# Block-causal attention and a maxout layer on one core: the rounding remainder of the weights taken by GpSimd, their loads issued by SyncE, two pairs of heads turned by TensorE

## The chip, the cores and the metric

The kernel runs on one core of a Trainium2 chip. The metric is the device time of one execution in microseconds (us). Before the change three runs gave 911.82, 914.31 and 915.15 us, median 914.31 us. Engines are named as in the profile: PE is TensorE, DVE is VectorE, ACT is ScalarE, POOL is GpSimd, SP is SyncE.

## The reference

Inputs are q, k, v of shape (8, 8, 576, 64) and four weight matrices. Attention is causal by blocks of 64 positions; its output, laid out as 4608 tokens of 512 numbers, goes through a layer that takes the largest of three products, and through an output product.

```python
scores = scale * np.matmul(q, k.transpose(0, 1, 3, 2))
scores = np.where(block_i >= block_j, scores, -1000000000.0)
attn = np.exp(scores - np.max(scores, axis=-1, keepdims=True))
attn = attn / (np.sum(attn, axis=-1, keepdims=True) + 1e-09)
out = np.matmul(attn, v)
x = out.transpose(0, 2, 1, 3).reshape(B * S, H * D)
h = np.maximum(np.maximum(x @ w1, x @ w2), x @ w3)
return (h @ w_out).astype(np.float32)
```

The weights arrive as 64-bit floats: each number is a low and a high 32-bit word. w1, w2, w3 are 512 x 768, w_out is 768 x 512.

## The kernel before, in words

**Attention.** Work goes by pairs of heads: 8 batches of 4 pairs. Batch 0 is done twice over, as FRONT pairs (the first 256 positions) and BACK pairs (the rest), so there are 36 pairs in all, numbered from 0 here. For each pair q and k are loaded into `nat`, turned so that the head dimension lies on the partitions (`kq`), multiplied (L934, and L941 for the last 64 rows), masked and reduced to a row minimum of the negated scores on DVE (L423), raised to the exponential on ACT (L607, L961), scaled by the inverse of the row sum on POOL or ACT (L441, L439), turned again (`pt` or `pz`), and multiplied with v (L1001). ACT and DVE copy the result out, ACT rounds it (`xh`), POOL takes the remainder (`xl`, through `minus`, L254).

There are two ways of turning. A *plain* pair (FRONT and BACK) is turned by PE: L825 for q and k, L559 and L987 for the probabilities, each a 128 x 128 transpose, and ACT or DVE copies the result out of PSUM (L251, L249). Any other pair (EARLY for batch 1, WHOLE for batches 2 to 7) is turned by DVE in blocks of 32 (L918 for q and k; L630 and L634 for the probabilities), and eight transfers of 200 KB on SP's queue (L642) bring the blocks to their partitions. The q and k of a pair that isn't plain are loaded in pieces of 32 numbers (L894); those of a plain pair in rows of 64 (L876, L882).

**Weights.** 24 units of 128 x 512 weights (18 of w1 to w3, 6 of w_out), class `Unit`, each turn 64-bit floats into a rounded part `h` and a remainder `l`. Per unit: POOL issues the load of 512 KB (L293). ACT takes the absolute value of the high words (`size`, L303). DVE does five steps: `clamp` L309, `shift` L316, `sign` L322, `power` L328 and `rest` L339. They give a float `a` from the high word and a correction `c` from the low word; `c` lies in a tile `left`, of which there is one, so a unit's `rest` must wait until the unit before has been used by PE. ACT rounds `a` to `h` (`high`). PE forms `a - h + c` in PSUM with three products by an identity (`whole`): L346 multiplies `plus`, read as 32-bit float, with `a`; L347 multiplies `less`, the negated identity, with `h`; L348 multiplies `plus` with `c`. ACT copies the sum to `l` (`lower`).

**Layer.** `Chunk` multiplies x with the weights for one half of a batch (256 or 320 columns). Each product is three matmuls (L1119: high x high, low x high, high x low); the maximum is taken on DVE (L1134); the output products are L1185, three matmuls of 512 columns each. Chunks follow each other; within the first one, each unit of weights gives PE 12 matmuls of 256 columns.

**Order of the work.** Nothing is ordered by hand at the engines. Each piece is a `Job` with an estimated cost for each engine that may do it, a rank, predecessors and slots of buffers; `in_order` plays the list through once, always starting the ready job of lowest rank on an idle engine, and writes the instructions in that order. On the chip each engine, SP's queue too, follows its written order and waits where an operand isn't there yet. A job that may run on two engines goes to the one that is free first by the estimates. So a changed cost or an added job moves others nearby.

**Issue of transfers.** Transfers issued by SP and ACT share eight semaphores in turn; each transfer waits until the one eight before it has landed. Transfers issued by POOL have semaphores of their own.

Of the kernel before, what the change touches and what calls it, by code (L numbers as in the profile page):

```python
# [9 lines left out]
F32 = mybir.dt.float32  # L10
F32R = mybir.dt.float32r
I32 = mybir.dt.int32
# [23 lines left out]
LOAD = 540.0  # L36
ASK = 1000.0
# [100 lines left out]
def pe(*cols, least=128):  # L138
    return sum(max(n, least) / 2.4 + 13.5 for n in cols)


def dve(n, fast=False):
    return 68.0 + n / (1.92 if fast else 0.96)


def act(n, psum=True):
    return (52.0 if psum else 88.0) + n / 1.2


def pool(n):  # L150
    return 150.0 + 2.15 * n
# [3 lines left out]
def kernel(  # L155
# [11 lines left out]
    nc = tc.nc  # L167
    B, H, S, D = q.shape
    DM, DF = w1.shape
    DO = w_out.shape[1]  # L170
    P = 128
    assert (S, D) == (576, 64) and H % 2 == 0
    NP = H // 2
# [14 lines left out]
    NEAR = 4  # L188
# [11 lines left out]
    const = ctx.enter_context(tc.tile_pool(name="const", bufs=1))  # L200
# [20 lines left out]


    plus = const.tile([P, P], F32R, name="plus")
    less = const.tile([P, P], F32R, name="less")
    one = att.tile([P, P], F32, name="p0", bufs=slots["p0"])
    make_identity(nc, one)
    nc.scalar.mul(less, one, -1.0)
    nc.scalar.copy(plus, one)

    wh, wl = {}, {}  # L230
# [8 lines left out]
    def job(cost, rank, call, *args, after=(), take=(), give=(), lasts=0.0, moved=0.0):  # L239
        j = Job(cost, rank, lambda eng: call(eng, *args), after, take, give, lasts, moved)  # L240
        jobs.append(j)
        return j
# [10 lines left out]
    def minus(eng, dst, a, b):  # L253
        {"DVE": nc.vector, "POOL": nc.gpsimd}[eng].tensor_tensor(out=dst, in0=a, in1=b, op=ALU.subtract)  # L254


    class Unit:


        def __init__(self, u, src, dst, n, prior, *early, first=None):  # L260
            self.src, self.dst, self.n, self.u = src, dst, n, u
            self.last = n == DO
            rank = DELAY + PACE * u


            self.tag = f"wo{dst}" if self.last else f"w{u}"
            self.temps = (f"wo{u % NF}",) if not self.last else (f"wo{4 + dst % 2}",) if dst < 4 else ("osb", "osb")
            j = self.issued = job(
                {"POOL": ASK},
                rank - 8,  # L270
                self.load,
                after=(prior and prior.issued, first, *(e.sized for e in early if e)),
                take=(self.tag,) if self.last else (),
            )
            j = job({}, 0, lambda eng: None, after=(j,), lasts=MOVE, moved=1600.0)
            j = self.sized = job({"ACT": act(512, False) + 65.0}, rank, self.size, after=(j,), take=self.temps)
            for step, fast in (
                (self.clamp, True),
                (self.shift, True),
                (self.sign, False),  # L280
                (self.power, True),
                (self.rest, False),
            ):
                c = dve(512, fast) + (130.0 if fast else 80.0)
                e = "DVE"
                j = job({e: c}, rank, step, after=(j,), take=("left",) if step == self.rest else (), lasts=c + GAP)
            j = job({"ACT": act(512, False)}, rank, self.high, after=(j,))
            j = job({"PE": 6 * pe(512)}, rank, self.whole, after=(j,), take=("pm",), give=(*self.temps, "left"))
            self.done = job({"ACT": act(512)}, rank, self.lower, after=(j,), give=("pm",))

        def load(self, eng):
            st = moe.tile([P, 1024], F32, name=self.tag, bufs=1).bitcast(I32)
            nc.gpsimd.dma_start(st.rearrange("p (c f) -> p c f", f=2 * self.n), self.src.bitcast(I32))  # L293
            lo_hi = st.rearrange("p (n t) -> p n t", t=2)
            self.low_word, self.high_word = lo_hi[:, :, 0].bitcast(U32), lo_hi[:, :, 1]

# [46 lines left out]
        def whole(self, eng):  # L343

            self.ps = psm.tile([P, 512], F32, name="pm")
            nc.tensor.matmul(self.ps, plus.bitcast(F32), self.a, start=True, stop=False)  # L346
            nc.tensor.matmul(self.ps, less, self.h, start=False, stop=False)  # L347
            nc.tensor.matmul(self.ps, plus, self.c, start=False, stop=True)  # L348

        def high(self, eng):  # L350
            w = moe.tile([P, 2, 512], F32R, name=self.tag, bufs=1)
            self.h, self.l = w[:, 0], w[:, 1]
            if self.last:
                woh[self.dst], wol[self.dst] = self.h, self.l
            else:
                wh[self.dst], wl[self.dst] = (t.rearrange("p (c f) -> p c f", f=P) for t in (self.h, self.l))
            copy(eng, self.h, self.a)
# [4 lines left out]
    units, begun = {}, []  # L362

    def weights():
        u, prior, early = 0, None, []
        for f in range(NF):
            for i, w in enumerate((w1, w2, w3)):
                prior = units[i, f] = Unit(
                    u, w[:, f * P : (f + 1) * P].rearrange("(c p) f -> p c f", p=P), (i, f), P, prior, early[u - NEAR] if u >= NEAR else None, first=begun[min(u + 1, NP - 1)]
                )  # L370
                early.append(prior)
                u += 1
        for f in range(NF):
            prior = units["out", f] = Unit(
                u,
                w_out[f * P : (f + 1) * P, :].rearrange("(c p) f -> p c f", p=P),
                f,
                DO,
                prior,
                early[2 * NF + f],  # L380
                early[u - 2],
            )
            early.append(prior)
            u += 1
# [7 lines left out]
    RUN = 400  # L392
# [20 lines left out]

    WHOLE = Part(((3,), (2, 0)), (1,), (1, 0), S, slice(0, S), slice(0, RUN), True)
    EARLY = Part(((3,), (2, 0)), (1,), (1, 0), S, slice(0, S), slice(0, RUN))

    FRONT = Part(((1, 0),), (), (0,), 256, slice(0, 256), slice(0, 96), plain=True)
    BACK = Part(((3,), (2,)), (), (1,), S, slice(256, S), slice(96, RUN), plain=True)
# [607 lines left out]
    left = {}  # L1026
# [186 lines left out]
    chunks, made = [], []  # L1213

    def plan(b, part, gap):
        nonlocal rank
        pairs = [Pair(b, hp, part, len(made) + hp) for hp in range(NP)]
        for p in pairs:
            p.plan(rank, made[-1] if made else None)
            made.append(p)  # L1220
            rank += gap
        return pairs

    rank = 0
    front = plan(0, FRONT, FRONT_PAIR)
    start = rank + SECOND + 6
    back = plan(0, BACK, BACK_PAIR)
    chunks.append((0, 0, front, start, rank + END))
    start, pairs = rank + END, {0: back}
    for b in range(1, B):  # L1230
        pairs[b] = plan(b, EARLY if b == 1 else WHOLE, PAIR)
        if b == 1:
# [4 lines left out]
        start = rank + END  # L1237
# [5 lines left out]
    prior = None  # L1243
    for b, half, pairs, start, end in chunks:
        prior = Chunk(b, half, pairs, prior, start, end)
# [33 lines left out]
```

## Time and profile before

| what | value |
|---|---|
| median of three runs | 914.31 us |
| the profiled execution | 913.83 us |
| its span, first to last instruction | 912.0 us |
| PE busy | 892.8 us, 98% |
| DVE busy | 529.3 us, 58% |
| ACT busy | 471.7 us, 52% |
| POOL busy | 254.8 us, 28% |
| weight loads, POOL's queue | 18 of w1 to w3 and 6 of w_out, 512 KB each |

The profile gives busy time by engine, the span cut into stretches, groups of equal instructions by line and shape, waits by releaser, and a chain of work followed back from the last instruction. A busy PE can still be late: matmuls are pipelined and a matmul's recorded length runs over the next one's start, so the pace of PE is read from start to start.

### The profile page before, as it was taken

The page shows a single profiled execution, that of the slowest core. Times are in us where ns is not written, and L with a number is a line of the kernel's source. Part 1 is how long each engine was busy: PE and PEld are TensorE (multiplying, and loading weights), DVE is VectorE, ACT ScalarE, POOL GpSimd, SP SyncE. Part 2 cuts the span into 40 slices and gives each one's busy share as a digit, 9 for nine tenths or more (in the row PEclk, how much of TensorE's full clock was granted, in tenths as well). Part 3 has the DMA queues.
Part 4 walks back from the last instruction along what each step waited for, and adds up shares of the span by engine and source line. Part 5 has one row for each costly group of instructions (what it writes and reads, how often), then busy time and mean ns, then how long its engine had stood idle before and what let it go on. Part 6 is the DMA issues. An engine that isn't in the chain of part 4 may idle for free.

```text
span 912.0 us, 16897 instructions
## 1 busy us (share of the span) xinstructions
PE 892.8 (98%) x5880; PEld 743.1 (81%) x5880; DVE 529.3 (58%) x1545; ACT 471.7 (52%) x1365; POOL 254.8 (28%) x381
## 2 busy tenths in 40 slices
PE   6999899999999999999999999999999999999998
PEld 4577677777888888888888888888888888899997
DVE  4999888786545756564555746564554756421111
ACT  3887675666544635545543645546553644522111
POOL 3553232243221312223221322233131322222100
PEclk9899999999999999999999999999999999999999
DMA  5772645776554544454554543555553533330010
GB/s 163 202 217 50 135 116 116 167 150 144 106 135 110 104 101 90 115 118 115 112 130 97 105 108 89 125 113 121 112 123 87 118 82 83 97 73 24 1 36 23
DMA packets 226132, 98.36 MB, mean 108 GB/s; under 512 B 189696, under 2 KB 218368, under 8 KB 226048
## 3 DMA queue, kind: packets, MB, share of 16 engines
q1 hardware_dynamic: 208192, 82.35, 40.6%
q0 software_dynamic: 3456, 12.58, 4.4%
q10 hardware_dynamic: 14400, 2.36, 1.4%
q8 instruction: 46, 0.75, 0.3%
q14 instruction: 38, 0.31, 0.1%
HBM read 41.94 MB, written 9.44 MB: 56 GB/s over the span
## 4 chain that ended last, share of the span: by engine, by line
PE 90%; DVE 5%; DMA 1%; ACT 1%; issue 1%; ACTq 0%; POOL 0%; DVEq 0%
PE pm L1119 50%; PE pm L1185 16%; PE sb L1001 10%; PE sb L934 8%; PE sb L941 3%; PE pm L346 1%; DMA nat<-in_q_dram 1%; DVE sb L423 1%; DVE left L339 1%; DVE wo L322 1%; PE sb L559 1%; DMA nat<-in_k_dram 0%; DVE kq L251 0%; ACT p L439 0%; PE pm L348 0%
## 5 line engine op out<-in xcount | busy, mean ns | idle before, releaser
L1119 PE MATMUL pm<-xh,w 128*128 128x320 f32 (+1 forms) x2304 | 498.6, 303 | 0.7 <-ACT xh L249 0.5
L1119 PEld LDWEIGHTS pm<-xh,w 128*128 128x128 f32 x2304 | 378.8, 189 | 18.8 <-issue 14.0
L1119 PE MATMUL pm<-xl,w 128*128 128x256 f32 (+1 forms) x1152 | 340.7, 296 | 0.5 <-DMA nat<-in_k_dram 0.5
L1119 PEld LDWEIGHTS pm<-xl,w 128*128 128x128 f32 x1152 | 218.5, 190 | 6.7 <-issue 5.3
L423 DVE CUSTOM_DVE_ANT_0 sb<-sb,mask 128x512 f32<-128x512 f32 (+3 forms) x288 | 143.7, 530 | 133.5 <-PE sb L941 76.1
L607 ACT ACTIVATE p<-sb,nm 128x256 f32<-128x256 f32 (+3 forms) x256 | 133.9, 527 | 80.2 <-DVE nm L423 73.7
L1134 DVE TENSOR_TENSOR m<-pm,m 128x256 f32<-128x256 f32 (+1 forms) x192 | 85.9, 448 | 147.9 <-PE pm L1119 147.1
L441 POOL TENSOR_TENSOR p<-p,rs 128x128 f32<-128x128 f32 (+4 forms) x133 | 97.9, 755 | 253.9 <-DVE rs L751 194.5
L630 DVE STREAM_TRANSPOSE pz<-p 128x512 f32<-128x512 f32 (+1 forms) x280 | 137.7, 527 | 36.0 <-ACT p L439 19.1
L254 POOL TENSOR_TENSOR hl<-m,hh 128x256 fp32r<-128x256 f32 x96 | 71.5, 745 | 248.4 <-ACT hh L249 216.5
L1185 PE MATMUL pm<-wo,hh 128*128 128x512 f32 x384 | 119.2, 392 | 0.0
L439 ACT ACTIVATE p<-p,rs 128x512 f32<-128x512 f32 (+4 forms) x155 | 88.2, 597 | 20.6 <-DVE rs L751 14.1
L249 ACT CAST hh<-m 128x256 fp32r<-128x256 f32 x96 | 38.8, 405 | 110.1 <-DVE m L1134 109.1
L934 PE MATMUL sb<-kq 64*128 64x256 f32 (+3 forms) x512 | 89.1, 466 | 3.2 <-DVE kq L251 3.1
L1001 PE MATMUL sb<-pt,vn 128*64 128x320 f32 (+4 forms) x840 | 90.2, 363 | 0.4 <-DVE pt L251 0.3
L254 POOL TENSOR_TENSOR xl<-x,xh 128x256 fp32r<-128x256 f32 (+1 forms) x64 | 52.7, 829 | 130.9 <-ACT xh L249 130.9
L1001 PEld LDWEIGHTS sb<-pt,vn 128*64 128x64 f32 x840 | 55.1, 137 | 34.5 <-issue 1.7
L1185 PEld LDWEIGHTS pm<-wo,hh 128*128 128x128 f32 x384 | 70.9, 188 | 14.9 <-issue 0.3
L934 PEld LDWEIGHTS sb<-kq 64*128 64x128 f32 x512 | 46.3, 192 | 38.1 <-issue 20.8
L1185 PE MATMUL pm<-wo,hl 128*128 128x512 f32 x192 | 74.9, 390 | 0.0
L249 ACT COPY osb<-pm 128x512 f32<-128x512 f32 x36 | 21.1, 587 | 69.5 <-PE pm L1185 67.4
L249 ACT COPY m<-pm 128x256 f32<-128x256 f32 (+1 forms) x96 | 38.1, 397 | 32.6 <-PE pm L1119 23.9
(82 smaller groups left out, 764.0 us busy)
## 6 DMA issues: line engine op xcount, KB each, us to landing
pt<-pz SPq DMA_DIRECT2D x224, 200.0 KB, 3.9
w<-in_moe_w_dram POOLq DMA_DIRECT2D x18, 512.0 KB, 5.2
vn<-in_v_dram SPq DMA_DIRECT2D x64, 128.0 KB, 2.4
out_dram<-osb SPq DMA_DIRECT2D x32, 256.0 KB, 2.0
nat<-in_k_dram SPq DMA_DIRECT2D x112, 72.0 KB, 2.4
nat<-in_q_dram SPq DMA_DIRECT2D x96, 72.0 KB, 2.5
wo<-in_moe_w_out_dram POOLq DMA_DIRECT2D x6, 512.0 KB, 4.4
nat<-in_q_dram ACTq DMA_DIRECT2D x16, 72.0 KB, 4.3
```

What stands on the lines that cost most here:

```text
L249: nc.scalar.copy(dst, src)
L254: {"DVE": nc.vector, "POOL": nc.gpsimd}[eng].tensor_tensor(out=dst, in0=a, in1=b, op=ALU.subtract)
L423: nc.vector.tensor_tensor_reduce(out=ps, in0=ps, in1=hidden, scale=-SCALE, scalar=first, op0=ALU.add, op1=ALU.min, accum_out=out_)
L439: nc.scalar.mul(p, p, r)
L441: nc.gpsimd.tensor_tensor(out=p, in0=p, in1=r.broadcast_to([P, p.shape[1]]), op=ALU.mult)
L607: nc.scalar.activation(dst, src, AF.Exp, bias=nm[:, c : c + 1], scale=-1.0, accum_out=sm[:, c : c + 1])
L630: nc.vector.transpose(dst, p[:, 0 : n * P])
L934: nc.tensor.matmul(ps, self.q[h.own, P * t : P * (t + 1)], self.k[h.own, 0:w], start=True, stop=True)
L1001: nc.tensor.matmul(o[h.own].rearrange("p (i u) -> p i u", u=n)[:, :, c0 : c0 + z - a], self.vn[:, kt, h.j, :], h.pt[:, :, h.off + a : h.of ...
L1119: nc.tensor.matmul(self.ps, w[i, f][:, c, :], xx, start=(c == 0 and s == 0), stop=(c == NC - 1 and s == 2))
L1134: nc.vector.tensor_tensor(out=m, in0=ps, in1=m, op=ALU.max)
L1185: nc.tensor.matmul(self.po[: self.rows], h, w[f], start=(f == 0 and s == 0), stop=(f == NF - 1 and s == 2))
```

## The change

Three edits, in `Unit`, in `weights` and in `plan`.

1. *Remainder.* A new step `remain` on POOL writes `l = a - h` (512 columns, operands in SBUF, through `minus`). PE's `whole` then has two products, `plus` with `l` and `plus` with `c`, both with operands of the rounded format; `plus` is no longer read as 32-bit float, and `less` is gone. `lower` writes the sum over `l` as before.
2. *Loads.* The 24 loads of weights are issued on SP's queue and no longer on POOL's. The planner charges them to SP at 540 ns. The first four are tied to fixed moments (1.5, 4.0, 6.5 and 9.0 us of the planner's time) and no longer to the loads of k of pairs 1 to 3.
3. *Pairs.* The first two pairs of batch 1 are plain (`FIRST`, the same division as `EARLY`), so that PE and not DVE turns them.

```diff
-    less = const.tile([P, P], F32R, name="less")
-    nc.scalar.mul(less, one, -1.0)
...
-                {"POOL": ASK},
+                {"SP": LOAD},
...
             j = job({"ACT": act(512, False)}, rank, self.high, after=(j,))
-            j = job({"PE": 6 * pe(512)}, rank, self.whole, after=(j,), take=("pm",), give=(*self.temps, "left"))
+            j = job({"POOL": pool(512)}, rank, self.remain, after=(j,))
+            j = job({"PE": 2 * pe(512)}, rank, self.whole, after=(j,), take=("pm",), give=(*self.temps, "left"))
...
-            nc.gpsimd.dma_start(st.rearrange("p (c f) -> p c f", f=2 * self.n), self.src.bitcast(I32))
+            nc.sync.dma_start(st.rearrange("p (c f) -> p c f", f=2 * self.n), self.src.bitcast(I32))
...
-            nc.tensor.matmul(self.ps, plus.bitcast(F32), self.a, start=True, stop=False)
-            nc.tensor.matmul(self.ps, less, self.h, start=False, stop=False)
+            nc.tensor.matmul(self.ps, plus, self.l, start=True, stop=False)
             nc.tensor.matmul(self.ps, plus, self.c, start=False, stop=True)
+
+        def remain(self, eng):
+
+            minus(eng, self.l, self.a, self.h.bitcast(F32))
...
-  early[u - NEAR] if u >= NEAR else None, first=begun[min(u + 1, NP - 1)]
+  early[u - NEAR] if u >= NEAR else None, first=job({}, 0, lambda eng: None, lasts=1500.0 + 2500.0 * u) if u < NEAR else None
...
+    FIRST = Part(((3,), (2, 0)), (1,), (1, 0), S, slice(0, S), slice(0, RUN), plain=True)
...
-        pairs = [Pair(b, hp, part, len(made) + hp) for hp in range(NP)]
+        pairs = [Pair(b, hp, FIRST if b == 1 and hp < 2 else part, len(made) + hp) for hp in range(NP)]
```

In the changed kernel line numbers are shifted by one to three: L345 and L346 are the products of `whole`, L292 is the load, L252 `minus`, L308, L315, L321, L327 and L338 the five steps on DVE, L828 the turning of q and k on PE.

SP's queue at the program's start, before. `nat` takes k, `vn_75` and `vn_76` take v of alternate pairs:

```order
L876 DMA nat<-in_k_dram 128x2x64 x2
L903 DMA vn_75<-in_v_dram 128x2x64 x2
L876 DMA nat<-in_k_dram 128x2x64 x2
L903 DMA vn_76<-in_v_dram 128x2x64 x2
L876 DMA nat<-in_k_dram 128x2x64 x4
L903 DMA vn_75<-in_v_dram 128x2x64 x2
```

The same place after; `w_100` is the tile of unit 0, `w_121` of unit 1 and so on:

```order
L879 DMA nat<-in_k_dram 128x2x64 x2
L906 DMA vn_75<-in_v_dram 128x2x64 x2
L292 DMA w_100<-in_moe_w_dram 128x4x256
L879 DMA nat<-in_k_dram 128x2x64 x2
L906 DMA vn_76<-in_v_dram 128x2x64 x2
L292 DMA w_121<-in_moe_w_dram 128x4x256
L292 DMA w_131<-in_moe_w_dram 128x4x256
L879 DMA nat<-in_k_dram 128x2x64 x2
L292 DMA w_159<-in_moe_w_dram 128x4x256
L292 DMA w_164<-in_moe_w_dram 128x4x256
L292 DMA w_190<-in_moe_w_dram 128x4x256
L879 DMA nat<-in_k_dram 128x2x64 x2
```

Six loads of weights now stand among the loads of k and v of the first four pairs; the k of pair 2 follows the loads of units 0 to 2, and further loads stand behind loads of v, which wait for PE to be done with the tile.

DVE's order before, from the inverse of the second pair's row sums to the end of unit 0's conversion (`wo_207` holds unit 0's `a`):

```order
L751 RECIPROCAL rs<-rs 128x2x2
L309 TENSOR_SCALAR wo_207<-wo_207 128x512
L251 COPY kq<-sb 128x2x256
L316 TENSOR_SCALAR wo_207<-wo_207 128x512
L322 SCALAR_TENSOR_TENSOR wo_207<-w_139,wo_207 128x512
L251 COPY pt<-sb 128x2x4x32
L328 TENSOR_SCALAR wo_207<-wo_207 128x512
L251 COPY pt<-sb 128x4x32
L423 ISA sb,nm<-sb,mask 128x256
L423 ISA nm 128x1
L339 SCALAR_TENSOR_TENSOR left<-w_139,wo_207 128x512
```

And after, the end of unit 0's conversion (`wo_151` holds its `a`, `wo_178` that of unit 1):

```order
L315 TENSOR_SCALAR wo_151<-wo_151 128x512
L308 TENSOR_SCALAR wo_178<-wo_178 128x512
L321 SCALAR_TENSOR_TENSOR wo_151<-w_100,wo_151 128x512
L249 COPY kq<-sb 128x2x256
L750 TENSOR_SCALAR rs<-sm 128x2x2
L327 TENSOR_SCALAR wo_151<-wo_151 128x512
L754 RECIPROCAL rs<-rs 128x2x2
L338 SCALAR_TENSOR_TENSOR left<-w_100,wo_151 128x512
L426 ISA sb,nm<-sb,mask 128x256
```

Unit 0 is now converted before the first row minimum of pair 2, and unit 1's first step stands inside it; before, unit 0 ended among the row minima of pair 3.

PE's order before, around the use of unit 1 (`wo_286`), with the scores of the first BACK pair (L934) and the product with v of pair 2 (L1001) ahead of it:

```order
L934 MATMUL sb<-kq 128x512 x2
L934 MATMUL sb<-kq 128x384 x2
L1001 MATMUL sb<-pz,vn_75 64x256 x2
L1001 MATMUL sb<-pz,vn_75 64x4x32 x2
L346 MATMUL pm<-wo_286,plus 128x512
L347 MATMUL pm<-w_416,less 128x512
L348 MATMUL pm<-left,plus 128x512
```

And after (`w_373` is unit 1's remainder from POOL):

```order
L1004 MATMUL sb<-pz,vn_75 64x256 x2
L1004 MATMUL sb<-pz,vn_75 64x4x32 x2
L828 MATMUL sb<-plus,nat 128x128 x7
L345 MATMUL pm<-w_373,plus 128x512
L346 MATMUL pm<-left,plus 128x512
L937 MATMUL sb<-kq 128x512 x2
L937 MATMUL sb<-kq 128x384 x2
```

Three products have become two, and unit 1 is used before the scores of that pair and no longer after them. Over the whole program PE has 68 more transposes, DVE two fewer of L918, 20 fewer of L630, 4 fewer of L634 and 24 more copies of L251, and SP 16 fewer transfers of L642.

More of the change, by code (lines that the diff above doesn't have):

```diff
@@ L368, in weights @@
                 prior = units[i, f] = Unit(
-                    u, w[:, f * P : (f + 1) * P].rearrange("(c p) f -> p c f", p=P), (i, f), P, prior, early[u - NEAR] if u >= NEAR else None, first=begun[min(u + 1, NP - 1)]
+                    u, w[:, f * P : (f + 1) * P].rearrange("(c p) f -> p c f", p=P), (i, f), P, prior, early[u - NEAR] if u >= NEAR else None, first=job({}, 0, lambda eng: None, lasts=1500.0 + 2500.0 * u) if u < NEAR else None
                 )
```

## The prediction

> **What bounds the kernel now.** I read the page first: who is busy, and what the chain of work that ended last is made of.
>
> ```profile
> PE 892.8 (98%) x5880; PEld 743.1 (81%) x5880; DVE 529.3 (58%) x1545; ACT 471.7 (52%) x1365; POOL 254.8 (28%) x381
> PE 90%; DVE 5%; DMA 1%; ACT 1%; issue 1%; ACTq 0%; POOL 0%; DVEq 0%
> ```
>
> Over the whole span PE is the limit. The shares are means, though, and the change touches only the part in which weights are converted. So the windows come next (us, then busy time and instructions of PE, PEld, DVE, ACT, POOL, the clock, DMA share and GB/s).
>
> ```profile
> 0.00:22.80 22.80, 13.95 (x62) 9.74 (x62) 9.61 (x39) 7.97 (x25) 8.74 (x22) 1.00 0.59 163
> 22.80:45.60 22.80, 20.55 (x96) 12.50 (x93) 21.12 (x62) 18.93 (x57) 11.86 (x19) 0.85 0.71 202
> 45.60:68.40 22.80, 22.53 (x143) 16.67 (x145) 21.32 (x51) 19.58 (x51) 12.81 (x16) 1.00 0.75 217
> 68.40:91.20 22.80, 22.75 (x142) 17.43 (x139) 22.18 (x54) 17.57 (x43) 8.28 (x9) 1.00 0.24 50
> 91.20:114.00 22.80, 20.14 (x122) 13.68 (x121) 18.64 (x42) 15.05 (x38) 6.36 (x9) 1.00 0.62 135
> 114.00:136.80 22.80, 22.80 (x137) 16.25 (x136) 19.01 (x54) 17.39 (x50) 6.98 (x8) 1.00 0.50 116
> 136.80:159.60 22.80, 22.36 (x126) 16.89 (x125) 20.30 (x60) 13.57 (x40) 4.61 (x6) 1.00 0.52 116
> 182.40:912.00 729.60, 725.05 (x4923) 622.25 (x4921) 380.60 (x1138) 347.16 (x1022) 189.07 (x286) 1.00 0.44 98
> ```
>
> Three stages differ. To 22.8 us nobody is full: a chain of first loads, scores and exponentials. From 22.8 to 91.2 us DVE is busy for 21.12 + 21.32 + 22.18 = 64.62 of 68.4 us and PE for 65.83: both are limits at once. From 91.2 to 159.6 us DVE is busy for 57.95 us and PE for 65.30. After 182.4 us PE stands still for 4.55 us in 729.6, and no part of the change is there. What can be won lies in the first 160 us.
>
> What fills DVE in the middle stage is the five steps of a unit (groups by shape, 22 to 91 us, mean ns before the last bar):
>
> ```profile
> L322 DVE SCALAR_TENSOR_TENSOR wo<-w,wo 128x512 int32<-128x512 int32 x16 | 11.4, 725 | 0.0
> L339 DVE SCALAR_TENSOR_TENSOR left<-w,wo 128x512 fp32r<-128x512 uint32 x14 | 10.3, 739 | 1.3 <-PE pm L348 1.3
> L316 DVE TENSOR_SCALAR wo<-wo 128x512 int32<-128x512 int32 x16 | 9.3, 596 | 0.0
> L309 DVE TENSOR_SCALAR wo<-wo 128x512 f32<-128x512 f32 x16 | 9.0, 576 | 0.2 <-ACT wo L303 0.2
> L328 DVE TENSOR_SCALAR wo<-wo 128x512 int32<-128x512 int32 x16 | 7.7, 483 | 0.0
> ```
>
> That is 47.7 of 64.62 us, or 3.1 us a unit. None of it is removed by the change.
>
> **The change part by part.** The sum is made against the profiled execution: 913.83 us, its span of 912.0 and 1.83 around it; that is 0.5 us under the median of 914.31.
>
> *The remainder, on PE.* PE's timeline shows a unit's products and what follows, then transposes (start, length).
>
> ```profile
> 105.49 1.02 PE L346 MATMUL pm<-wo,plus 128*128 128x512 f32 x2
> 105.99 0.75 PE L347 MATMUL pm<-w,less 128*128 128x512 f32 x1
> 106.58 0.40 PE L348 MATMUL pm<-left,plus 128*128 128x512 f32 x1
> 106.81 0.28 PE L1119 MATMUL pm<-xh,w 128*128 128x256 f32 x1
> ...
> 111.58 1.09 PE L559 MATMUL sb<-plus,p 128*128 128x128 f32 x7 [0.42 <-ACT p L439]
> 112.50 0.71 PE L987 MATMUL sb<-plus,p 128*128 128x128 f32 x5
> 112.97 0.36 PE L1119 MATMUL pm<-xh,w 128*128 128x256 f32 x1
> ```
>
> From start to start a unit takes 106.81 - 105.49 = 1.32 us. L348, one product of the rounded format, takes 106.81 - 106.58 = 0.23. Two such remain, 0.46, so PE is relieved of 0.86 us a unit: 24 x 0.86 = 20.6 us.
>
> *The two pairs, on PE.* 68 transposes are added. Twelve take 112.97 - 111.58 = 1.39 us, 0.116 each, so 7.9 us. Net relief of PE: 12.7 us. If PE alone set the end, that would be the gain.
>
> *The two pairs, on DVE.* The groups over the whole span give what goes; two copies out of PSUM, from 22 to 91 us, bound what comes.
>
> ```profile
> L630 DVE STREAM_TRANSPOSE pz<-p 128x512 f32<-128x512 f32 (+1 forms) x280 | 137.7, 527 | 36.0 <-ACT p L439 19.1
> ...
> L634 DVE STREAM_TRANSPOSE pz<-p 128x128 f32<-128x128 f32 x56 | 15.1, 269 | 0.0
> L918 DVE STREAM_TRANSPOSE kq<-nat 128x1152 f32<-128x1152 f32 x28 | 38.1, 1361 | 3.4 <-DMA nat<-in_q_dram 3.1 <-PE sb L934 0.2
> ...
> L251 DVE COPY pt<-sb 128x256 f32<-128x256 f32 x5 | 2.1, 416 | 0.0
> L251 DVE COPY kq<-sb 128x512 f32<-128x512 f32 x3 | 2.0, 674 | 0.0
> ```
>
> 20 x 0.527 + 4 x 0.269 + 2 x 1.361 = 14.3 us leave DVE. 24 copies come to it, at 0.416 to 0.674, so 10.0 to 16.2 us: between -4.3 and +1.9. I take -2, since copies of both sizes are among them. The rest goes to ACT, which has 3 to 5 us free in each window. So DVE is hardly relieved, and the 3.1 us a unit stay.
>
> *The remainder, on POOL.* A subtraction of 512 columns isn't in the trace. It is bounded by a product of 512 columns, and by the subtractions of 256 and 320 columns. The load that leaves POOL stands below them:
>
> ```profile
> L441 POOL TENSOR_TENSOR p<-p,rs 128x512 f32<-128x512 f32 x27 | 29.2, 1087 | 4.6 <-PE sb L1001 4.3 <-DVE rs L751 0.4
> L254 POOL TENSOR_TENSOR hl<-m,hh 128x256 fp32r<-128x256 f32 x96 | 71.5, 745 | 248.4 <-ACT hh L249 216.5 <-ACT left L249 31.7
> L254 POOL TENSOR_TENSOR xl<-x,xh 128x320 fp32r<-128x320 f32 x32 | 29.2, 914 | 119.8 <-ACT xh L249 119.8
> ...
> L293 POOL DMA_DIRECT2D w<-in_moe_w_dram x18 | 14.5, 808 | 0.0
> ```
>
> From 1.09 to 0.914 + 3 x (0.914 - 0.745) = 1.42 us; I take the middle, 1.25. POOL gets 24 x 1.25 = 30 us and loses some 24 x 0.81; in its fullest window it was busy for 12.81 of 22.8 us, so its own time is covered. What isn't covered is what it does to DVE. The same step of DVE, alone and beside POOL:
>
> ```profile
> 19.50 0.40 DVE L309 TENSOR_SCALAR wo<-wo 128x512 f32<-128x512 f32 x1
> ...
> 66.53 1.90 DVE L309 TENSOR_SCALAR wo<-wo 128x512 f32<-128x512 f32 x2
> ```
>
> ```profile
> 66.05 3.28 POOL L441 TENSOR_TENSOR p<-p,rs 128x384 f32<-128x384 f32 x3 [1.44 <-DVE rs L751]
> ```
>
> 0.40 us alone, 0.95 each beside POOL. Against 0.40, the means of 0.576, 0.596 and 0.483 above cost 16 x (0.176 + 0.196 + 0.083) = 7.3 us in the middle stage, while POOL was busy for 32.95 us, loads among it: 0.22 us per us. The 16 units of that stage add 20 us of POOL and take away 13, so +1.5 us for DVE if a load counts like a subtraction; if loads count for nothing, 7.3 / (32.95 - 13) x 20 = +7.3. I take +2, since slowed steps are seen beside loads as well. The Trainium skill ("SBUF — State Buffer", Who interferes with whom) says that a DVE instruction in a two-port mode, or with two SBUF inputs, and a GpSimd instruction that reads SBUF shut each other out for the whole instruction. The rows agree in kind; by that rule at its worst the term would be 20 and not 2.
>
> PE's first product of a unit now waits for POOL, and behind it in PE's order stand that unit's matmuls and the next pair's scores. The way from ACT's rounding to PE's end is 1.25 longer by POOL and 0.86 shorter by PE; with one tile `left`, the next `rest` waits for all of it. 0.4 us more, against 3.1 of DVE work a unit, is covered, unless POOL's queue holds a scaling ahead of it: then 1.09 more.
>
> *The loads, on SP.* What each queue showed: SP's longest wait (us, times, longest), the first conversion's steps, and the second load of q for the third pair on ACT's queue.
>
> ```profile
> SPq L903 <- PE sb L1001: 61.3, 6, 22.0
> ...
> 16.33 0.66 ACT L303 ACTIVATE wo<-w 128x512 f32<-128x512 f32 x1
> ...
> 24.80 0.69 DVE L339 SCALAR_TENSOR_TENSOR left<-w,wo 128x512 fp32r<-128x512 uint32 x1
> ...
> 9.58 0.43 ACTq L876 DMA_DIRECT2D nat<-in_q_dram  x1
> ```
>
> Unit 0 was converted at 24.80 us, while DVE had been idle for 13.2 of the first 22.8. By the changed order unit 0 and a step of unit 1 stand ahead of the third pair's row minima; 1.1 units at 3.1 us are at best 3.5 us moved into idle time. Against that, six loads of 0.5 MB come among the first k and v, where 163 GB/s were already moved (2.5 us a load at the 202 to 217 of the next windows), and ACT's loads of q share semaphores with them; ACT stands still while its queue waits. That loses 0 to 4 us. I take -2 for the start, between -3.5 and +4. Unit 6's load is the first behind a v that waits for PE; it is needed six units, 18.6 us of DVE, after unit 0's, so I take nothing for it.
>
> *Fewer transfers.* The first pair that DVE turned waited long for its q:
>
> ```profile
> 91.58 6.70 DMA nat<-in_q_dram
> 98.56 1.38 DVE kq L918
> ```
>
> That wait is on the chain, and PE was busy for only 20.14 us of that window. The first two pairs of batch 1 no longer meet it; a later pair may. I take half, -3.4.
>
> *The sum by stages.* Start: -2. Middle: DVE's 3.78 us of idle time are all that PE's relief can win there; half of it, -1.9, with +2 from POOL: 0. Third stage: PE loses 8 x 0.86 = 6.9 and gains 7.9, +1; DVE -2 and +0.9, on which PE waits in part, -1; the wait -3.4: together -3.4. Total -5.4: 913.83 - 5.4 = 908.4 us. Of PE's 12.7 us the larger part is spent waiting for DVE, which is late next.
>
> **The rivals.**
>
> *PE's relief arrives in full.* For it: PE 90% of the chain, and DVE's copies can go to ACT. Then -12.7: 901.1 us (897 to 904). Against it: 64.62 of 68.4 us of DVE, with nothing taken from it before the pairs of batch 1. Chance 0.22.
>
> *Nothing is left of it.* SP's order decides: weights behind v that waits for PE (61.3 us in six waits, 22.0 the longest), and the first q later, so that the start gives +2 where I took -2, and the wait for q only passes to the next pair (0 for -3.4). 908.4 + 4 + 3.4 = 915.8, say 912 to 918. Against it: v's loads wait because they come early. Chance 0.15.
>
> *Slower, by POOL holding DVE.* In the middle stage DVE wants one of the five steps 47.7 / 64.62 = 74% of the time. If each subtraction stops DVE for its whole 1.25 us, the middle gets 20 instead of 2: 926.4 us. It counts as slower from 0.78 us a unit on, (10.5 + 2) / 16. For it: 0.95 against 0.40. Against it: the mean of L309 was 0.576 beside a POOL that was busy for half of the stage, 32.95 of 68.4 us. Chance 0.13. By the rule of the Trainium skill named above this is what happens whenever POOL is first and DVE wants one of the steps.
>
> **How the numbers follow.** A measurement of this kernel can tell about 0.5%, 4.6 us, from no change: faster is under 909.7, slower over 918.9. My forecast has 0.50; its own range is 903 to 914 (start up to +4 or -3.5, middle -3.8 to +5), and of it 0.31 lies under 909.7, 0.19 above. Faster: 0.31 + 0.22 = 0.53. Same: 0.19 + 0.15 = 0.34. Slower: 0.13. The range goes from 899, into the first rival, to 917, to the end of the second, and leaves out the last and a tip of the first.
>
> **What would show it.** Right: DVE busy for over 66 us of 22.8 to 91.2 us, PE for some 10 less than before; L345 waiting for POOL for less than 0.5 us at a time; unit 0's `rest` (L338) before 22 us; the five steps' means up by less than 0.1 us; the last `whole` between 145 and 152 us. Wrong: PE still full in the middle stage and the last `whole` before 140 us (first rival); ACT or DVE waiting for a load of weights, or for q, for more than 2 us (second); the two-operand steps and L308 near 1 us in the mean (third). After 182 us PE's idle time must stay near 4.6 us; if it grows, the two pairs have been paid for elsewhere, and the sum is wrong in a place where I put nothing.

## The result, and the profile after

The changed kernel took 921.43 us, the median of five runs (917.73 to 924.26), against 914.31 before. The ratio is 1.0079, with a 95% interval of 1.0059 to 1.0100: slower by 7 us, by more than the 0.5% that a measurement can tell. The forecast was 908.4, with a range of 899 to 917. The profiled execution took 919.79 us, its span was 918.0.

The page of the changed kernel, the shares and the chain:

```profile
PE 888.3 (97%) x5900; PEld 743.0 (81%) x5900; DVE 537.5 (59%) x1543; ACT 477.0 (52%) x1375; POOL 269.4 (29%) x378
PE 87%; DVE 6%; ACT 2%; issue 1%; DMA 1%; POOL 1%; ACTq 1%; SPq 0%; DVEq 0%; POOLq 0%
```

In net PE lost 48 instructions of the weights and got 68 transposes (5880 + 20 = 5900). Its share of the chain fell from 90% to 87%: work went away, and waiting came. The windows say where (us; busy time of PE, PEld, DVE, ACT, POOL; clock; DMA share; GB/s):

```profile
0.00:22.80 22.80, 14.18 (x57) 9.21 (x58) 11.65 (x46) 11.62 (x35) 6.21 (x17) 1.00 0.85 247
22.80:45.60 22.80, 17.81 (x89) 10.67 (x87) 20.31 (x56) 15.81 (x47) 10.05 (x11) 0.83 0.54 140
45.60:68.40 22.80, 21.87 (x149) 17.51 (x147) 20.94 (x49) 17.52 (x46) 11.82 (x12) 0.95 0.68 194
68.40:91.20 22.80, 17.81 (x104) 12.86 (x101) 22.46 (x46) 15.65 (x38) 10.00 (x8) 0.93 0.09 26
91.20:114.00 22.80, 19.51 (x139) 14.98 (x138) 21.56 (x48) 18.16 (x45) 11.79 (x10) 1.00 0.37 98
114.00:136.80 22.80, 21.93 (x143) 16.75 (x143) 21.79 (x56) 19.05 (x53) 12.00 (x13) 1.00 0.39 100
136.80:159.60 22.80, 22.63 (x154) 17.07 (x151) 18.95 (x51) 16.28 (x48) 10.67 (x14) 1.00 0.44 98
182.40:918.00 735.60, 730.30 (x4944) 625.92 (x4940) 383.69 (x1150) 349.72 (x1028) 188.59 (x285) 1.00 0.44 98
```

In the middle stage, 22.8 to 91.2 us, PE is busy for 17.81 + 21.87 + 17.81 = 57.49 us, where it was 65.83. DVE is as full as before, 63.71 against 64.62. After it DVE is full for longer: 43.35 us of the two windows from 91.2 to 136.8, where it was 37.65. What DVE did in the middle stage shows in the groups of 22 to 91 us (count; busy us, mean ns):

```profile
L321 DVE SCALAR_TENSOR_TENSOR wo<-w,wo 128x512 int32<-128x512 int32 x13 | 10.8, 828 | 0.0
L308 DVE TENSOR_SCALAR wo<-wo 128x512 f32<-128x512 f32 x13 | 10.2, 786 | 0.0
L338 DVE SCALAR_TENSOR_TENSOR left<-w,wo 128x512 fp32r<-128x512 uint32 x12 | 9.0, 752 | 1.4 <-PE pm L346 1.3
L327 DVE TENSOR_SCALAR wo<-wo 128x512 int32<-128x512 int32 x13 | 8.5, 656 | 0.0
L315 DVE TENSOR_SCALAR wo<-wo 128x512 int32<-128x512 int32 x14 | 7.3, 524 | 0.0
L426 DVE CUSTOM_DVE_ANT_0 sb<-sb,mask 128x512 f32<-128x512 f32 x9 | 6.2, 692 | 0.6 <-PE sb L944 0.6
```

The five steps take nearly the same DVE time as before (45.8 us against 47.7; the last row is the masked reduction, for later), but 13 units instead of 16. DVE is full, and each unit costs it more: L308 went from 576 to 786 ns, L327 from 483 to 656, L321 from 725 to 828. The new instruction on POOL, from the groups of the first 160 us:

```profile
L252 POOL TENSOR_TENSOR w<-wo,w 128x512 fp32r<-128x512 f32 x18 | 26.3, 1462 | 28.1 <-ACT w L247 24.9 <-DMA wo<-in_moe_w_out_dram 3.2
```

It takes 1.46 us where I had 1.25. The start and the end of the conversion, from the timeline (start, length): unit 0's `rest`, and the last unit's last product.

```profile
19.24 0.69 DVE L338 SCALAR_TENSOR_TENSOR left<-w,wo 128x512 fp32r<-128x512 uint32 x1
...
161.10 0.39 PE L346 MATMUL pm<-left,plus 128*128 128x512 f32 x1
```

Unit 0 is 5.6 us earlier than before (24.80), as its earlier load promised. The last unit is outside the 145 to 152 us that I forecast, on the late side: before, it came at 150.71, and in e5 below, the same order without the subtraction, at 148.77.

### The profile page after: what moved, and what is told of

Same layout as the page of the kernel before. It is cut to its first block, busy times and chain, and to the rows that moved or that the text cites. A ratio compares the mean times of both kernels' runs of the same rounds, so it can differ in the third digit from the quotient of the medians.

```text
span 918.0 us, 16954 instructions
## 1 busy us (share of the span) xinstructions
PE 888.3 (97%) x5900; PEld 743.0 (81%) x5900; DVE 537.5 (59%) x1543; ACT 477.0 (52%) x1375; POOL 269.4 (29%) x378
## 4 chain that ended last, share of the span: by engine, by line
PE 87%; DVE 6%; ACT 2%; issue 1%; DMA 1%; POOL 1%; ACTq 1%; SPq 0%; DVEq 0%; POOLq 0%
PE pm L1122 48%; PE pm L1188 16%; PE sb L1004 10%; PE sb L937 8%; PE sb L944 3%; DVE sb L426 1%; DVE left L338 1%; DVE wo L321 1%; PE sb L562 1%; DVE wo L327 1%; DVE wo L308 1%; DMA nat<-in_k_dram 1%; ACT p L610 0%; DMA pt<-pz 0%; ACT w L247 0%
## 5 line engine op out<-in xcount | busy, mean ns | idle before, releaser
L1137 DVE TENSOR_TENSOR m<-pm,m 128x256 f32<-128x256 f32 (+1 forms) x192 | 85.9, 448 | 145.3 <-PE pm L1122 144.4
L444 POOL TENSOR_TENSOR p<-p,rs 128x128 f32<-128x128 f32 (+4 forms) x128 | 93.4, 748 | 244.3 <-DVE rs L754 181.8
L633 DVE STREAM_TRANSPOSE pz<-p 128x512 f32<-128x512 f32 (+1 forms) x260 | 127.8, 528 | 35.5 <-ACT p L442 19.3
L252 POOL TENSOR_TENSOR hl<-m,hh 128x256 fp32r<-128x256 f32 x96 | 72.9, 759 | 233.0 <-ACT hh L247 201.2
L442 ACT ACTIVATE p<-p,rs 128x256 f32<-128x256 f32 (+4 forms) x160 | 91.3, 599 | 15.4 <-DVE rs L754 9.3
L252 POOL TENSOR_TENSOR xl<-x,xh 128x256 fp32r<-128x256 f32 (+1 forms) x64 | 52.6, 828 | 115.2 <-ACT xh L247 111.8
L1004 PEld LDWEIGHTS sb<-pt,vn 128*64 128x64 f32 x812 | 52.7, 138 | 34.2 <-issue 1.9
L937 PEld LDWEIGHTS sb<-kq 64*128 64x128 f32 x512 | 45.8, 192 | 40.8 <-issue 21.3
```

Source lines behind the costliest of these rows:

```text
L442: nc.scalar.mul(p, p, r)
L444: nc.gpsimd.tensor_tensor(out=p, in0=p, in1=r.broadcast_to([P, p.shape[1]]), op=ALU.mult)
L633: nc.vector.transpose(dst, p[:, 0 : n * P])
L937: nc.tensor.matmul(ps, self.q[h.own, P * t : P * (t + 1)], self.k[h.own, 0:w], start=True, stop=True)
L1004: nc.tensor.matmul(o[h.own].rearrange("p (i u) -> p i u", u=n)[:, :, c0 : c0 + z - a], self.vn[:, kt, h.j, :], h.pt[:, :, h.off + a : h.of ...
L1137: nc.vector.tensor_tensor(out=m, in0=ps, in1=m, op=ALU.max)
```

## The experiments

Three theories were set against each other. Theory 1: POOL's subtraction, reading the same memory, takes time from DVE's five steps. Theory 2: the loads on SP spoil the start. Theory 3: the two pairs put more on PE than they take away. Times below are medians; "against before" is the difference to the median of the kernel before on the same chip.

**One edit alone, and two without the first.** Of the diff of the change, e1 has only edit 1 (remainder), e2 only edit 2 (loads), e3 only edit 3 (pairs), e4 edits 2 and 3. As a sample, the whole of e2:

```diff
-                {"POOL": ASK},
+                {"SP": LOAD},
-            nc.gpsimd.dma_start(st.rearrange("p (c f) -> p c f", f=2 * self.n), self.src.bitcast(I32))
+            nc.sync.dma_start(st.rearrange("p (c f) -> p c f", f=2 * self.n), self.src.bitcast(I32))
-  first=begun[min(u + 1, NP - 1)]
+  first=job({}, 0, lambda eng: None, lasts=1500.0 + 2500.0 * u) if u < NEAR else None
```

> The kernel before with the remainder on POOL alone: two products on PE a unit, loads still issued by POOL, no further plain pairs. Theory 1 (POOL's subtraction shuts DVE out of its five steps): slower than before, 917 to 927 us, with L309, L316 and L328 at 0.65 us or more in the mean from 22 to 160 us, although PE has 20.6 us less to do. Theory 2 (the loads on SP spoil the start and hold up q): faster, 898 to 908 us. Theory 3 (the two pairs put too much on PE and ACT): faster, 898 to 908 us.

> The kernel before with the loads of the weights on SP's queue alone. Theory 1: near the kernel before or somewhat faster, 908 to 915 us, since POOL is relieved of 18 us of issuing. Theory 2: slower, 919 us or more, with ACT or DVE waiting for q or for a load. Theory 3: near the kernel before.

> The kernel before with the first two pairs of batch 1 turned by PE alone. Theory 1: within 5 us of the kernel before, 909 to 919 us; PE has 7.9 us more to do, but DVE's wait of 6.7 us for q goes. Theory 2: the same. Theory 3: slower, 919 us or more.

> The changed kernel without the remainder on POOL: loads on SP and two plain pairs, PE forming the remainder in three products as before. Theory 1: faster than the changed kernel by 5 us or more, 906 to 916 us, with the five steps of DVE back near 0.42 and 0.68 us. Theory 2 and theory 3: as slow as the changed kernel or slower, 920 to 932 us, since PE has 20.6 us more to do.

| kernel | us | ratio, 95% interval | against before |
|---|---|---|---|
| e1, remainder alone | 932.20 | 1.0206 (1.0183 to 1.0229) | +18.9 |
| e2, loads alone | 909.87 | 0.9961 (0.9947 to 0.9976) | -3.5 |
| e3, pairs alone | 919.93 | 1.0061 (1.0039 to 1.0083) | +6.6 |
| e4, loads and pairs | 917.18 | 1.0037 (1.0024 to 1.0050) | +3.8 |

Theory 2 falls: the loads on SP win 3.5 us and beat the kernel before. Theory 1 has the right sign in e1, but 932.20 is more than its 917 to 927: this order has a loss of its own, as e12 shows below. L308 and L315 took 701 and 668 ns there, as asked, L327 only 495. e4 is 4.3 us faster than the changed kernel, a little under the 5 that theory 1 asked for, and just over its 906 to 916. Theory 3 holds for the pairs by themselves. The windows of e3 show why:

```profile
91.20:114.00 22.80, 22.32 (x142) 16.52 (x141) 20.45 (x49) 17.38 (x45) 8.98 (x11) 1.00 0.45 129
114.00:136.80 22.80, 22.49 (x140) 16.54 (x139) 18.41 (x51) 17.17 (x48) 7.52 (x10) 1.00 0.37 94
136.80:159.60 22.80, 22.80 (x144) 17.64 (x143) 14.54 (x42) 15.34 (x47) 2.95 (x5) 1.00 0.42 85
159.60:182.40 22.80, 22.80 (x157) 18.88 (x157) 16.11 (x48) 12.49 (x41) 6.93 (x11) 1.00 0.33 56
```

From 91.2 us on PE is full, busy for 22.32 us of the window in which it was busy for 20.14 before. The wait for q is gone, but PE is given 7.9 us of transposes in a place where it has no time for them. And e2, which leaves the pairs to DVE, has this:

```profile
91.20:114.00 22.80, 22.42 (x136) 15.68 (x136) 20.54 (x48) 15.54 (x41) 5.60 (x7) 1.00 0.53 115
114.00:136.80 22.80, 22.80 (x130) 16.40 (x127) 21.51 (x63) 16.20 (x44) 4.91 (x8) 1.00 0.52 119
```

22.42 us: with the loads alone PE's gap in that window has closed as well. There was nothing left in it for the pairs to win.

**What of the remainder costs: PE's new wait or POOL's hold on DVE.** In the next three the changed kernel's order is kept. e5 leaves POOL's subtraction out; e6 lets it write into a tile that nobody reads; e7 puts two fills in its place, so that POOL still stands between ACT and PE but reads nothing. In e5 and e6 PE multiplies `h` where it multiplied `l`.

```diff
 e5
-            nc.tensor.matmul(self.ps, plus, self.l, start=True, stop=False)
+            nc.tensor.matmul(self.ps, plus, self.h, start=True, stop=False)
-            minus(eng, self.l, self.a, self.h.bitcast(F32))
+            pass
 e6, the product as in e5
-            minus(eng, self.l, self.a, self.h.bitcast(F32))
+            minus(eng, spare, self.a, self.h.bitcast(F32))
 e7, the product as in the changed kernel
-            minus(eng, self.l, self.a, self.h.bitcast(F32))
+            nc.gpsimd.memset(self.l.bitcast(F32), 0.0)
+            nc.gpsimd.memset(self.l.bitcast(F32), 0.0)
```

> The changed kernel, POOL's subtraction left out; PE multiplies the rounded part h where it multiplied l (the output is that of a computation without the remainder). PE keeps its relief of 0.86 us a unit. Theory 1 (the subtraction on POOL costs what PE gains): the run comes to 917.2, the time of loads and pairs together, less 12 to 20.6 us of PE: 897 to 905 us; PE nearly full from 45 us on; the five steps of DVE back to the means of before (0.48 to 0.74 us). Rival A (PE's relief is worth nothing, since DVE is full anyway): 914 to 919 us, with DVE over 63 us busy from 22.8 to 91.2 us and PE under 60.

> The changed kernel with POOL's subtraction going into a tile that nobody reads; PE multiplies h where it multiplied l (the remainder is left out of the output). POOL works as in the changed kernel, but PE does not wait for it. Theory 1a (POOL takes DVE's time while it subtracts): 916 to 922 us, as the changed kernel, and the five steps of DVE as slow as there (0.66 to 0.83 us in the middle stage). Theory 1b (the way from ACT over POOL to PE is too long for one tile of corrections): 897 to 906 us, as without the subtraction. Half of each: near 911.

> The changed kernel with two fills of 512 columns in place of POOL's subtraction: POOL still stands between ACT and PE, for about 1 us a unit, but reads no operand (the remainder is left out of the output). Theory 1a (two operands read by POOL shut DVE out): 897 to 906 us and DVE's five steps at the means of before. Theory 1b (the way is too long): 914 to 921 us, with PE waiting for POOL as in the changed kernel.

e5 took 908.33 us (ratio 0.9951, 0.9933 to 0.9969), e6 921.05 (1.0088, 1.0068 to 1.0108), e7 912.97 (0.9995, 0.9981 to 1.0008). e6 takes as long as the changed kernel though PE doesn't wait for POOL's result; what is left of its wait at that product is for ACT's rounding (us, times, longest):

```profile
PE pm L346 <- ACT w L248: 0.4, 2, 0.2
```

So the wait costs less than these runs can tell (their intervals are some 2 us either way), and the subtraction by being there costs 921.05 - 908.33 = 12.7 us. e5 itself lies between its two forecasts, 897 to 905 and 914 to 919: PE's relief counts, but for less than theory 1 gave it. The groups of DVE's three one-operand steps in e5, to 190 us, with one of the two-operand steps above them:

```profile
L321 DVE SCALAR_TENSOR_TENSOR wo<-w,wo 128x512 int32<-128x512 int32 x18 | 14.3, 794 | 0.0
...
L308 DVE TENSOR_SCALAR wo<-wo 128x512 f32<-128x512 f32 x22 | 11.9, 540 | 0.2 <-ACT wo L302 0.2
...
L327 DVE TENSOR_SCALAR wo<-wo 128x512 int32<-128x512 int32 x22 | 10.2, 464 | 0.0
...
L315 DVE TENSOR_SCALAR wo<-wo 128x512 int32<-128x512 int32 x22 | 9.2, 418 | 0.0
```

The same in e6, where lines are one higher, with POOL's subtraction from the same stretch below:

```profile
L328 DVE TENSOR_SCALAR wo<-wo 128x512 int32<-128x512 int32 x22 | 16.1, 731 | 0.0
...
L309 DVE TENSOR_SCALAR wo<-wo 128x512 f32<-128x512 f32 x22 | 15.3, 697 | 0.3 <-ACT wo L303 0.2
...
L316 DVE TENSOR_SCALAR wo<-wo 128x512 int32<-128x512 int32 x22 | 12.2, 554 | 0.0
```

```profile
L253 POOL TENSOR_TENSOR spare<-wo,w 128x512 fp32r<-128x512 f32 x18 | 24.4, 1353 | 27.6 <-ACT w L248 27.6
```

Two meetings from e6's timeline (L316 is `shift`, L309 `clamp`, L427 the masked reduction), and below them `clamp` with no subtraction beside it, from e5's:

```profile
32.59 0.42 DVE L316 TENSOR_SCALAR wo<-wo 128x512 int32<-128x512 int32 x1
32.64 1.50 POOL L253 TENSOR_TENSOR spare<-wo,w 128x512 fp32r<-128x512 f32 x1 [2.07 <-ACT w L248]
...
32.92 1.50 DVE L309 TENSOR_SCALAR wo<-wo 128x512 f32<-128x512 f32 x1
...
139.57 1.27 POOL L253 TENSOR_TENSOR spare<-wo,wo 128x512 fp32r<-128x512 f32 x1
139.72 0.70 DVE L427 CUSTOM_DVE_ANT_0 sb<-sb,mask 128x512 f32<-128x512 f32 x1 [0.91 <-PE sb L938]
```

```profile
68.50 0.41 DVE L308 TENSOR_SCALAR wo<-wo 128x512 f32<-128x512 f32 x1
```

`shift` came 0.05 us ahead of POOL and kept its 0.42 us; POOL's subtraction, second, took 1.50 in place of 1.27; `clamp`, behind it, took 1.50 in place of 0.41 and ended at 34.42, 0.28 after POOL. The reduction at 139.72, which takes scores from PSUM, was not touched (0.70 beside POOL; 0.69 in the groups of the changed kernel), and did not touch POOL. Of the 24 subtractions of e6, 17 have one of the five steps beside them that takes 0.8 us or more. The Trainium skill ("SBUF — State Buffer", Who interferes with whom) says that whichever of the two engines issues first has the shared ports for its whole instruction, and that the other is stopped and not slowed. These rows agree in kind; POOL's 0.23 us more are less than the 0.37 for which `shift` still ran.

e7 lies between. POOL's fills, and the same three steps, to 190 us:

```profile
L308 DVE TENSOR_SCALAR wo<-wo 128x512 f32<-128x512 f32 x22 | 14.5, 658 | 0.2 <-ACT wo L302 0.2
L321 DVE SCALAR_TENSOR_TENSOR wo<-w,wo 128x512 int32<-128x512 int32 x18 | 14.0, 780 | 0.0
...
L327 DVE TENSOR_SCALAR wo<-wo 128x512 int32<-128x512 int32 x22 | 11.0, 499 | 0.0
L315 DVE TENSOR_SCALAR wo<-wo 128x512 int32<-128x512 int32 x22 | 10.8, 493 | 0.0
```

```profile
L351 POOL MEMSET w<- 128x512 f32 x18 | 10.9, 606 | 1.0
L350 POOL MEMSET w<- 128x512 f32 x18 | 10.3, 573 | 19.1 <-DVE left L338 19.1
```

The fills hold POOL for 1.18 us a unit, not much less than a subtraction, and cost 912.97 - 908.33 = 4.6 us. So a busy POOL, and a PE that waits for it, are not the price. The one-operand steps are slower than in e5 (36.3 us against 31.3); the two-operand step L321 isn't (780 ns against e5's 794). The other one, L338, has some long instructions in e7 too (up to 1.26 us), and those stand beside POOL's other work, which reads, and not beside a fill. Reading nothing is cheaper, but not free, which theory 1a had not expected.

**Twice the subtraction.** e9 is e6 with the subtraction written twice.

```diff
             minus(eng, spare, self.a, self.h.bitcast(F32))
+            minus(eng, spare, self.a, self.h.bitcast(F32))
```

> As the kernel whose subtraction nobody waits for, but POOL subtracts twice for each unit (the remainder is left out of the output). Theory 1a (POOL takes DVE's time while it subtracts): the second subtraction costs what the first did, 12.7 us, so 931 to 937 us, and DVE's excess over the lone times of its five steps rises by some 12 to 15 us again. If the first cost came from the order of the jobs or from something else that is already there: 920 to 924 us.

It took 932.59 us (1.0202, 1.0185 to 1.0218): 10.4 us more than e6, each against its own kernel before, where 12.7 were expected. DVE's five steps rise by 10.1, where 12 to 15 were. Its rows, to 190 us:

```profile
L328 DVE TENSOR_SCALAR wo<-wo 128x512 int32<-128x512 int32 x22 | 18.2, 826 | 0.0
L309 DVE TENSOR_SCALAR wo<-wo 128x512 f32<-128x512 f32 x22 | 16.3, 740 | 0.3 <-ACT wo L303 0.2
L316 DVE TENSOR_SCALAR wo<-wo 128x512 int32<-128x512 int32 x22 | 16.2, 735 | 0.0
```

The next table sets the time beside what DVE spent on all five steps of all 24 units, the sum of the twelve groups by shape of which the rows above are the largest. The work is the same in each kernel. The steps are those of one profiled execution of each; e6's was its slowest, 925.10 us.

| kernel | five steps, us | against before, us |
|---|---|---|
| e5, no subtraction | 70.9 | -5.0 |
| e7, fills | 76.4 | -0.3 |
| the changed kernel | 84.5 | +7.1 |
| e6, subtraction beside | 85.9 | +7.8 |
| e9, twice beside | 96.0 | +18.1 |

From e5 to e9 DVE spends 25.1 us more, and the kernel takes 23.1 more. What POOL takes from DVE arrives in the end almost one for one. This is the cause of the loss, shown by dose.

One companion of it was not separated. PE's granted clock, the column of the windows where 1.00 is full, was 1.00 in all three windows from 22.8 to 91.2 us of e5, but 0.93, 1.00 and 0.93 in e6, 0.83, 0.95 and 0.93 in the changed kernel, and 0.93, 1.00 and 0.85 in e9. Weighted with PE's busy time in these windows, that is 2.4, 5.4 and 3.4 us, an estimate of the most that it can have added to PE's work. e6 loses as much as the changed kernel with less than half of it, so it is not what the loss goes by in the main; how much of the loss passes through it stays open.

**What PE's relief is worth.** e8 is the changed kernel without the two pairs, e10 the same without POOL's subtraction as well, and e12 is e1 without it.

```diff
 e8 and e10, against the changed kernel (e12: edits 2 and 3 undone)
-        pairs = [Pair(b, hp, FIRST if b == 1 and hp < 2 else part, len(made) + hp) for hp in range(NP)]
+        pairs = [Pair(b, hp, part, len(made) + hp) for hp in range(NP)]
 e10 and e12 besides, as in e5
-            nc.tensor.matmul(self.ps, plus, self.l, start=True, stop=False)
+            nc.tensor.matmul(self.ps, plus, self.h, start=True, stop=False)
-            minus(eng, self.l, self.a, self.h.bitcast(F32))
+            pass
```

> Remainder on POOL and loads on SP, without the two pairs turned by PE. If the parts add up to the changed kernel: 921 less the 6 to 7 us that the pairs cost alone: 914 to 916 us. If the remainder costs here what it cost alone (19 us, less the 3.5 that the loads win): 926 to 930 us, and then the pairs are a gain of 6 or more once the remainder is there. If the pairs cost only where PE is full, and here it is not: 919 to 922.

> Loads on SP and PE's relief alone: no two pairs turned by PE, and POOL's subtraction left out (PE multiplies h where it multiplied l, the remainder is left out of the output). If PE's relief is worth 8.9 us here as beside the two pairs: 901 us. If DVE is the limit and PE's 7.9 us for the two pairs fit into its slack: 907 to 910 us, the same as with the pairs. If PE's relief counts in full: 889 to 893.

> The remainder's edit alone, loads issued by POOL as before, with POOL's subtraction left out (PE multiplies h where it multiplied l). With the subtraction this came to 932 us, 11 more than with the loads on SP. If that is the price of a subtraction that shares POOL's queue with the loads: 905 to 912 us. If the order that the planner makes with the loads on POOL is bad by itself: 917 to 922 us.

e8 took 921.12 us (1.0085, 1.0069 to 1.0101), +7.8 against before: the same as with the pairs. e10 took 910.72 (0.9962, 0.9948 to 0.9975), -3.7, where the loads alone gave -3.5: PE's 20.6 us of relief bring nothing there, in the order that the planner makes with them. From e4 to e5, with the pairs, the relief is worth 8.8 us (+3.8 to -5.0). In these orders the relief pays for the pairs' 7.9 us and for no more. The windows of e10 show what stops it in the middle stage:

```profile
22.80:45.60 22.80, 18.54 (x118) 12.16 (x116) 21.97 (x64) 19.07 (x56) 8.78 (x11) 1.00 0.67 174
45.60:68.40 22.80, 21.19 (x146) 16.33 (x145) 21.47 (x53) 18.62 (x45) 5.77 (x6) 1.00 0.61 182
68.40:91.20 22.80, 18.63 (x125) 13.58 (x123) 21.91 (x52) 17.00 (x42) 5.09 (x5) 1.00 0.36 84
```

DVE is busy for 65.35 of 68.4 us, PE for 58.36. Nothing is left there for PE to be faster at. That is not the whole of it: e11 below is faster than e10 with the relief of six units only, and e10's PE also has gaps from 136.8 to 159.6 us, where it is busy for 19.98 of 22.8. What part of that is the order was not separated.

e12 took 921.47 us (1.0079, 1.0062 to 1.0096), +7.0 against before, where e1 had +18.9. So the subtraction costs about the same in that order too, 11.9 us. But the remainder's edit without its subtraction is 7 us slower than before when POOL issues the loads, with no more DVE time in the five steps (72.4 us by the same sum; before 73.1). The planner makes another order there, in which PE has gaps late:

```profile
114.00:136.80 22.80, 20.03 (x128) 15.29 (x126) 20.24 (x57) 16.80 (x46) 5.86 (x8) 1.00 0.54 112
136.80:159.60 22.80, 19.91 (x104) 13.79 (x104) 21.30 (x60) 14.00 (x38) 5.33 (x8) 1.00 0.56 148
```

Which job's new place makes these gaps was not tried. It is no part of the changed kernel, whose loads are SP's.

**A faster version.** If the relief helps only where PE is full, the subtraction should be kept for the units that are converted there. e11 is e2 with the remainder on POOL for the six units of w_out alone.

```diff
+            if self.last:
+                j = job({"POOL": pool(512)}, rank, self.remain, after=(j,))
-            j = job({"PE": 6 * pe(512)}, rank, self.whole, ...
+            j = job({"PE": (2 if self.last else 6) * pe(512)}, rank, self.whole, ...
```

> Loads on SP alone, and the remainder on POOL for the last six units (those of w_out) only, which are converted from 100 to 142 us, where PE is full and DVE has 1 to 6 us free in each 22.8. PE is relieved of 6 x 0.86 = 5.2 us there; at the average price of a subtraction so far (12.7 / 24 = 0.53 us) POOL costs 3.2: 907 to 909 us, against 909.9 with the loads alone. If PE's relief counts and POOL's hold is covered there: 904 to 906. If each of POOL's subtractions costs its whole 1.46 us: 913 us.

It took 907.90 us (0.9932, 0.9918 to 0.9946), 6.6 less than before and the fastest that gives the whole result. The intervals of e2 (from 0.9947) and e11 (to 0.9946) just don't meet: the step between them is small. By the sum of the table above DVE's five steps take 73.0 us, 2.8 more than in e2 for six subtractions, 0.47 each. Two windows:

```profile
91.20:114.00 22.80, 22.05 (x142) 15.94 (x144) 20.48 (x44) 15.44 (x40) 7.69 (x9) 1.00 0.53 113
114.00:136.80 22.80, 21.17 (x130) 16.49 (x129) 21.53 (x56) 13.59 (x38) 8.12 (x10) 1.00 0.49 117
```

PE is no longer full from 114 us (22.80 in e2), at the same DVE time (21.51 there).

## Why the prediction was wrong

**The step that failed.** It is the term of the remainder on POOL: "I take +2, since slowed steps are seen beside loads as well", with 0.9 more in the third stage. Measured: 12.7, and DVE's five steps took 15.0 us more. The mechanism was named, as the third rival, and given 0.13; the size was wrong. Two reasons are shown, and a third that lay near is not.

- *The rate.* I divided DVE's excess by all of POOL's busy time, loads among it, and got 0.22 us per us. The loads count for little: without them on POOL, in e2, the five steps take 70.2 us instead of 73.1, which is 0.12 us a load, though in another order of the work. The 24 subtractions take 85.9 - 70.9 = 15.0. Over e6's 24 x 1.37 us, all groups of the subtraction together, that is 0.46 us per us.
- *The number.* I charged 16 units of the middle stage at 1.25 us, and took 0.9 us for the other 8 together. The length was right for a subtraction that no step holds up (1.27), but all 24 count, since DVE becomes full from 91 to 137 us as well. My own upper bound, with loads counted as nothing, has 7.3 / (32.95 - 13) = 0.37 us per us; over 24 x 1.37 = 33 us that is 12, close to what was measured.
- *The meetings, not shown.* I spread POOL's time evenly over DVE's. The subtraction starts when ACT has rounded, and 17 of 24 hit one of the five steps, most often `power` or `clamp`; the mean of `power` rose most, from 464 to 731 ns. But 17 of 24 is 71%, and the steps' share of DVE's busy time in the middle stage was 74% by my own figure. So these counts don't show that the order of the work brings the two together more often than chance. They fit that figure, which I had used for the third rival and not for the sum.

**The rest of the sum.** Without POOL's term I had -5.4 - 2.9 = -8.3 us; e5 gives -5.0.

- *Start, -2.* Unit 0's `rest` ran at 19.24 us, as forecast. e2, which has the loads and nothing else of the change, wins 3.5; how much of that is won at the start was not separated.
- *Middle, -1.9 from PE's relief.* DVE is late next, as I said, and the relief without the pairs brought nothing (-3.5 in e2, -3.7 in e10), so even half was too much.
- *The wait for q, -3.4.* It was too large from the start: 6.70 us is how long the transfer was on the chain, while DVE stood still for q for only 2.4 us there, 3.1 in all by the row of L918 in the prediction, and PE for 2.66 us in that window for whatever reason. And it was counted for the pairs, but the loads alone close PE's gap in that window (e2, 22.42 us), where DVE no longer waits for q. It could be won once only.
- *The pairs, +1 against the relief.* Near: +6.6 alone, where PE is full; beside the relief no clear difference (-3.7 in e10, -5.0 in e5, with intervals that overlap).
- *PE's new wait for POOL, nothing.* The largest row of PE's waits in the changed kernel (us in total, times, longest) exceeds the 0.5 us at a time that I allowed:

```profile
PE pm L345 <- POOL w L252: 4.7, 5, 1.7
```

  But it cost nothing measurable (921.43 us, and 921.05 in e6, which has no such wait).

**The signs.** I asked for DVE above 66 us in the middle stage; it was 63.71. PE came 8.3 lower, where I had said some 10. The five steps' means were to rise by less than 0.1 us; L308 rose by 0.21 and L327 by 0.17. The third rival's sign, L308 and the two-operand steps near 1 us, was half there: 786, 828 and 752 ns. Its point of decision, 0.78 us a unit, was too high: 12.7 / 24 = 0.53 was enough, because all units paid and the gains to set against it were smaller. PE's idle time after 182 us is 735.60 - 730.30 = 5.30, against 4.55: nothing was moved there. The first rival fell with e5 and e10, which have PE's relief without the subtraction and win 5.0 and 3.7 us. The second fell with e2, though its sign was there: ACT waited for a load of q for more than the 2 us that I had set. Before, the same wait was 2.0 us, and in e2, which is faster, 3.3.

```profile
ACT p L610 <- DMA nat<-in_q_dram: 2.5, 1, 2.5
```

## What to carry to other kernels

Work moved to GpSimd is not free because GpSimd is idle: if its operands lie in SBUF and DVE is full, count a good part of each of its instructions as DVE's time, and look at which DVE instruction will be running just then. Relief of an engine is worth something only in the windows where that engine, and not its neighbour, is full; here the one place where it was seen to pay by itself was that of six units of 24, and by 2 to 3 us. A wait that two edits would remove can be won once.

## What was not expected of the hardware

- A fill by POOL, which reads nothing, slows DVE too: 1.18 us of fills a unit made the three one-operand steps 5.0 us longer in all (36.3 against 31.3), while the two-operand step L321 stayed as it was (780 against 794 ns). The Trainium skill, in the section named above, has the same division: two-operand steps meet only what reads.
- What DVE does decides what it pays. Beside POOL's subtraction a step with operands in SBUF waits until POOL is nearly done or done (1.50 for 0.41 us, ended 0.28 after POOL), while the masked reduction of scores in PSUM runs through (0.70 us).
- It goes both ways: POOL's 512 columns took 1.27 us beside a reduction, 1.50 where `shift` had begun first, and 1.46 in the mean of the changed kernel.
